# Expert layers: weights stationary in the first layer of two-tile units, plain transposes and a VectorE sum for half tiles

## The chip, the cores and the metric

The kernel runs on one core of one Trainium2 chip. The metric is the device time of one execution in microseconds (us), as the median of several runs. The engines are TensorE (PE, with its weight loads shown as PEld), VectorE (DVE), ScalarE (ACT), GpSimd (POOL) and SyncE (SP, which here only issues DMAs).

## The reference, cut to what matters

Three stages run one after another: clustered attention, a dense layer with a PReLU, and a mixture of eight experts. Only the last is touched:

```python
def _moe2_ref(x, w_skip, w_gate, w1, w2):
    do_compute = x @ w_skip > 0
    xc = x[do_compute]
    e_idx = np.argmax(xc @ w_gate, axis=1)          # one expert per token
    ...
    for e in range(E):                              # E = 8, w1[e]: 512x1024, w2[e]: 1024x512
        mask = e_idx == e
        h = np.maximum(xc[mask] @ w1[e], 0.0)
        y[mask] = gate_w[mask, None] * (h @ w2[e])
    out[do_compute] = xc + y                        # the other tokens keep x
```

## The kernel before

**Precision.** Every fp32 operand of a large matmul is split into a high part and a low part (tiles that end in `h` and `l`), and a product is three matmuls: high by high, high by low, low by high. The split of a weight chunk is a ScalarE copy (`Weights.hi`, L1453) and then a VectorE subtraction (`Weights.lo`, L1457), each over 128x2048 elements. The low part of an activation is made in the same way: ScalarE writes the high part, VectorE subtracts.

**Units and tiles.** Tokens are sorted by expert and cut into units. A unit shares the four weight chunks of one expert: c = 0 and 1 are the two 512-column halves of the first layer, chunks 2 and 3 those of the second layer. In the order of work there are ten units, 0 to 9, with 16 tiles: a full tile has 128 tokens, a half tile 64. Units 2, 4 and 6 hold two full tiles (tiles 3 and 4, 6 and 7, 9 and 10). Units 1, 3 and 5 hold one half tile (tiles 2, 5, 8), units 0, 7 and 9 a full and a half one (the half ones are tiles 1, 12, 15), unit 8 one full one. A further block of nine units follows under a condition that these inputs do not meet.

**One tile.** Written as function calls, with t the tile and c the half:

- `transx(t)`: four TensorE transposes of the gathered rows `xg` into a PSUM bank `pt` (L1152, L1159 for half tiles), a ScalarE copy to the high part, a VectorE subtraction to the low part. In a half tile, high and low stand side by side in one 128-column operand, so that two groups of matmuls do instead of three, and the two halves of the result have to be added.
- `first(t, c)`: `group` (L1197) issues 12 matmuls (8 for a half tile). The token tile is the stationary operand and the weights move, 512 columns each; the result `h` has tokens on its partitions. ScalarE then writes `hb` (L1226).
- `transh(t, c)`: `hb` is transposed for the second layer. A full tile takes four transposes (L1242), a ScalarE copy `hTh` (L1243) and a VectorE subtraction `hTl` (L1250). A half tile takes four fp32 matmuls with the constant `two`, which transpose and add the two halves at once (L1238; the profile shows each as two instructions), a ScalarE relu (L1239) and a VectorE step (L1247).
- `second(t, c)`: 12 matmuls (8) with `hT` stationary into `yo`; after c = 1 the output is scaled and scattered.

**What sets the order.** Nothing reorders the instructions: each engine has its own queue and works through it in the order in which the code is written. `begin` writes out units 0 to 2 by hand, interleaved with the last part of the routing; `run` writes the rest by a rule. A turn is one `first` or `second`. At the start of a turn `ahead` converts one more weight chunk if one of the five slots is free (a `hi` on ACT, a `lo` on DVE) and has POOL issue the load of that chunk for the unit after the next. Then come the matmuls, then `transh` of the turn before, then the `transx` of the next unit. For a unit of one tile the turns are first(0), first(1), the first turn of the next unit, second(0), second(1):

```python
            if use and wsp.slots and n > 1:
                ahead()
            if c < 2:
                first(t, c)
            else:
                second(t, c - 2)
            while wait:
                transh(*wait.pop(0))
            if c < 2:
                wait.append((t, c))
```

**PSUM.** The pool `t` has three banks in rotation (transposes use it), `h` two, `y` two. A write into a bank waits until the last reader of its former contents is through.

Of the kernel before, what the change touches and what calls it, by code (L numbers as in the profile page):

```python
# [8 lines left out]
F32 = mybir.dt.float32  # L9
F32R = mybir.dt.float32r  # L10
# [16 lines left out]
DM = H * D  # L27
# [16 lines left out]
HALF = P // 2  # L44
# [25 lines left out]
TILES, UNIT, COLS = _plan()  # L70
# [15 lines left out]
HT = 4  # L86
# [1081 lines left out]
def moe2(ctx, tc, A, cst, R, y1d, wsp, wk, op, ps, x0, route, room):  # L1168
    nc = tc.nc
    ident = cst["ident"]  # L1170
    KD = DM // P
    xg, xT, hb, hT, yo, hp, more = {}, {}, {}, {}, {}, {}, []
    for t in range(2):
        xg[t], xT[t] = x0[0][t], (x0[1][0], x0[1][1:])[t]

    def gather(t):

# [29 lines left out]
    def is_half(t):  # L1207
        return TILES[t][2] < P

    def transx(t):  # L1210
        pt = ps["t"].tile([P, 4, P], F32, tag="t", name="pt")
        xT[t] = [wk.tile([P, 4, P], F32R, tag=f"xT{y}", name=f"xT{y}") for y in "hl"]
        if not is_half(t):
            transpose_x(nc, ident, xg[t], pt, *xT[t])
            return
        transpose_half(nc, ident, xg[t], pt, xT[t][0], TILES[t][1])

    def first(t, c, ks=range(4)):
        n = TILES[t][0]
        if ks[0] == 0:  # L1220
            hp[t, c] = ps["h"].tile([P, DM], F32, tag="h", name="h")
        group(hp[t, c], xT[t], wsp.w[n, c], is_half(t), True, True, ks)
        if ks[-1] == KD - 1:
            done(n, c)
            r = wk.tile([P, DM], F32, tag="hb", name="hb")
            nc.scalar.activation(r, hp.pop((t, c)), AF.Copy if is_half(t) else AF.Relu)  # L1226
            hb[t, c] = r

    def transh(t, c, late=None):
        pt = ps["t"].tile([P, 4, P], F32, tag="t", name="pt")  # L1230
        r = hb.pop((t, c))
        a = wk.tile([P, 4, P], F32R, tag="hTh", name="hTh", bufs=HT)
        b = wk.tile([P, 4, P], F32R, tag="hTl", name="hTl", bufs=HT)
        hT[t, c] = (a, b)
        if is_half(t):

            for k in range(4):
                nc.tensor.matmul(pt[:, k, :HALF], lhsT=r[:, k * P:(k + 1) * P], rhs=R["two"], start=True, stop=True)  # L1238
            nc.scalar.activation(a[:, :, :HALF], pt[:, :, :HALF], AF.Relu)  # L1239
        else:  # L1240
            for k in range(4):
                nc.tensor.transpose(pt[:, k], r[:, k * P:(k + 1) * P], ident)  # L1242
# [114 lines left out]
    def run(n0, n1, fresh=False):  # L1357


        tiles = {n: list(UNIT[n]) for n in range(n0, n1)}  # L1360
        F = {n: [(t, c) for c in range(2) for t in tiles[n]] for n in tiles}
        turns = []
        for n in range(n0, n1):
            if fresh or n > n0:
                turns += F[n]
            if len(tiles[n]) == 1 and 1 < n < n1 - 1:
                turns.append(F[n + 1].pop(0))
            if n + 1 < n1:
                turns += [(t, 2 + c) for c in range(2) for t in tiles[n]]
            else:  # L1370

                turns += [(t, 2 + c) for t in reversed(tiles[n]) for c in range(2)]
        use = []
        for t, c in turns:
            if (TILES[t][0], c) not in use and (TILES[t][0], c) not in wsp.w:
                use.append((TILES[t][0], c))

        def ahead():
            n, c = use.pop(0)
            wsp.take(n, c)  # L1380
            wsp.hi(n, c)
            wsp.lo(n, c, nc.vector)
            if n + 2 < n1:
                loadw(n + 2, c)

        last = UNIT[n1 - 1][-1] + 1
        if fresh:
            for t in range(UNIT[n0][0], UNIT[n0][0] + sum(XG)):
                gather(t)
            for n in (n0, n0 + 1):  # L1390
                for c in range(NPC):
                    loadw(n, c)
            for t in tiles[n0]:
                transx(t)
        wait = []
        for t, c in turns:
            n = TILES[t][0]
# [10 lines that stand above are left out]
            if c < 2 and n + 1 < n1:  # L1408

                if len(tiles[n]) == 1:  # L1410
                    rows = tiles[n + 1][c:c + 1]
                else:
                    rows = tiles[n + 1] if (t, c) == (tiles[n][-1], 1) else ()
                for t2 in rows:
                    transx(t2)
            if use and wsp.slots and n == 1:
                ahead()
            if c == 3:
                finish(t)
                if t + sum(XG) < last:  # L1420
                    gather(t + sum(XG))
# [39 lines left out]
def kernel(ctx, tc, A):  # L1461
    nc = tc.nc
# [4 lines left out]
    ident = cp.tile([P, P], F32, name="ident")  # L1467
# [20 lines left out]
    R = {}  # L1488
# [5 lines left out]
    def setup(sp):  # L1494
# [116 lines left out]
    wsp = Weights(nc, A, slots, raw)  # L1611
# [19 lines left out]
    def more():  # L1631
        rp2 = ctx.enter_context(tc.tile_pool(name="rawp2", bufs=1, reuse_waits="tile"))
        raw.extend(rp2.tile([P, 2048], F32, name=f"raw{c}") for c in (2, 3))
        R["pool"] = rp2

        pre = [rp2.tile([P, 2048], F32, tag=f"pre{c}", name=f"pre{c}") for c in range(NW)]
        for f in range(3, DFF // P):
            w32[f] = pre[(f - 2) // 2][:, (f % 2) * 2 * DM:(f % 2 + 1) * 2 * DM]
        xg = [rp2.tile([P, DM + 1], F32, name=f"xg{t}") for t in range(2)]
        place = iter(range(NW // 2))  # L1640

        def last():
# [17 lines left out]
        return fwk, fck, ps_y, wsp, slot, last, even, xg, setup  # L1660
# [16 lines left out]
    ps = {}  # L1677
# [60 lines left out]
```

## Time and profile before

| what | value |
|---|---|
| runs | 735.36 us median of 3 (734.87 to 736.76) |
| profiled execution, its own time | 735.44 us |
| its span (first to last instruction) | 733.5 us |
| PE busy | 707.3 us (96%) |
| DVE busy | 566.0 us (77%) |
| ACT busy | 477.9 us (65%) |
| expert stage | from about 532 us to the end of the span |

The span is what the profile shows; the 1.9 us between it and the execution's own time lie outside. Busy shares are averages over stages with different limits, so the expert stage has to be read by itself. In a timeline each row is one instruction or several equal ones that follow each other: start, length, engine, line, operation, tile written and tiles read, shapes, count, and in brackets how long the engine stood idle before it and what ended that.

### The profile page before, as it was taken

The page shows a single profiled execution, that of the slowest core. Times are in us where ns is not written, and L with a number is a line of the kernel's source. Part 1 is how long each engine was busy: PE and PEld are TensorE (multiplying, and loading weights), DVE is VectorE, ACT ScalarE, POOL GpSimd, SP SyncE. Part 2 cuts the span into 40 slices and gives each one's busy share as a digit, 9 for nine tenths or more (in the row PEclk, how much of TensorE's full clock was granted, in tenths as well). Part 3 has the DMA queues.
Part 4 walks back from the last instruction along what each step waited for, and adds up shares of the span by engine and source line. Part 5 has one row for each costly group of instructions (what it writes and reads, how often), then busy time and mean ns, then how long its engine had stood idle before and what let it go on. Part 6 is the DMA issues. An engine that isn't in the chain of part 4 may idle for free. (4 is left out here: it accounts for less than half of the span.)

```text
span 733.5 us, 11633 instructions
## 1 busy us (share of the span) xinstructions
PE 707.3 (96%) x4022; PEld 623.9 (85%) x4022; DVE 566.0 (77%) x1110; ACT 477.9 (65%) x916; POOL 375.0 (51%) x340
## 2 busy tenths in 40 slices
PE   9999999999999999999999999999999999999993
PEld 6988999889999899888889999998888778888872
DVE  5989888798989877888875989875478887775731
ACT  5878898788899955554446555656446676665620
POOL 4649778797796386666660000001127776583101
PEclk9999999999999999999999999999999999999997
DMA  7876668576656133333306200142618896867000
GB/s 210 226 170 170 125 134 198 146 176 128 172 144 155 52 110 126 116 115 115 115 0 210 93 2 0 58 109 111 241 44 314 313 404 247 321 226 304 18 10 25
DMA packets 46162, 109.22 MB, mean 149 GB/s; under 512 B 10779, under 2 KB 26587, under 8 KB 40721
## 3 DMA queue, kind: packets, MB, share of 16 engines
q1 hardware_dynamic: 39024, 67.81, 34.2%
q0 software_dynamic: 7072, 40.60, 14.7%
q8 instruction: 34, 0.56, 0.3%
q14 instruction: 32, 0.25, 0.1%
HBM read 74.78 MB, written 10.10 MB: 116 GB/s over the span
## 5 line engine op out<-in xcount | busy, mean ns | idle before, releaser
L341 DVE TENSOR_TENSOR etl<-pt,eth 128x384 fp32r<-128x384 f32 x192 | 102.2, 550 | 21.8 <-ACT eth L340 20.3
L340 ACT CAST eth<-pt 128x384 fp32r<-128x384 f32 x192 | 91.1, 486 | 20.4 <-PE pt L338 20.4
L338 PE MATMUL pt<-ident,e 128*128 128x128 f32 x576 | 93.7, 272 | 0.3 <-ACT e L327 0.3
L320 DVE TENSOR_REDUCE nm<-s 128x1 f32<-128x768 f32 x96 | 90.5, 943 | 3.2 <-PE s L307 2.9
L1165 POOL DMA_INDIRECT xg<-y1d,gi x16 | 26.3, 1646 | 130.1 <-DVE gi L1014 113.8
L327 ACT ACTIVATE e<-s,nm 128x768 f32<-128x768 f32 x96 | 87.5, 911 | 4.4 <-DVE nm L320 3.7
L695 ACT CAST gh<-gm 128x384 fp32r<-128x384 f32 x60 | 30.8, 514 | 82.0 <-DVE gm L693 58.5
L338 PEld LDWEIGHTS pt<-ident,e 128*128 128x128 f32 x576 | 73.6, 140 | 7.0 <-ACT e L327 0.5
L697 DVE TENSOR_TENSOR gl<-gm,gh 128x384 fp32r<-128x384 f32 x60 | 49.4, 823 | 25.7 <-ACT gh L695 25.1
L356 PE MATMUL px<-etl,vh 128*64 128x384 f32 (+1 forms) x192 | 65.7, 369 | 1.1 <-DVE etl L341 0.9
L304 PE MATMUL s<-AB 128*128 128x384 f32 x192 | 57.5, 380 | 2.3 <-ACT e L327 2.0
L667 PE MATMUL h<-xh,wh 128*128 128x384 f32 x256 | 55.8, 339 | 0.6 <-DVE gm L690 0.4
L667 PE MATMUL h<-xh,wl 128*128 128x384 f32 x256 | 56.0, 339 | 0.0
L567 POOL TENSOR_TENSOR pre<-ct,pre 128x512 int32<-128x512 int32 x26 | 37.2, 1453 | 35.9 <-DVE ct L565 35.9
L1285 POOL DMA_INDIRECT out_dram<-o,si x16 | 20.5, 1280 | 68.4 <-DVE o L1280 40.4
L667 PE MATMUL h<-xl,wh 128*128 128x384 f32 x256 | 55.0, 336 | 0.0
L358 PE MATMUL px<-eth,vh 128*128 128x384 f32 x160 | 53.9, 337 | 0.0
L1457 DVE TENSOR_TENSOR wl<-raw,wh 128x2048 fp32r<-128x2048 f32 (+2 forms) x26 | 44.3, 1712 | 11.6 <-ACT wh L1453 11.3
L307 PE MATMUL s<-CD 128*128 128x384 f32 x192 | 49.4, 338 | 1.0 <-DMA CD<-st 1.0
L667 PEld LDWEIGHTS h<-xh,wh 128*128 128x128 f32 x256 | 45.6, 188 | 3.3 <-DVE gm L690 0.5
L667 PEld LDWEIGHTS h<-xh,wl 128*128 128x128 f32 x256 | 44.6, 188 | 2.6 <-POOL wl L639 2.5
L667 PEld LDWEIGHTS h<-xl,wh 128*128 128x128 f32 x256 | 45.8, 188 | 0.0
(344 smaller groups left out, 1836.7 us busy)
## 6 DMA issues: line engine op xcount, KB each, us to landing
AB<-RL SPq DMA_DIRECT2D x32, 384.0 KB, 5.2
raw<-in_w_in_dram SPq DMA_DIRECT2D x16, 512.0 KB, 4.0
raw<-in_w_out_dram SPq DMA_DIRECT2D x16, 512.0 KB, 4.8
raw<-in_wall_dram SPq DMA_DIRECT2D x8, 1024.0 KB, 8.1
Tp<-in_qkT_dram SPq DMA_DIRECT2D x16, 384.0 KB, 3.7
CD<-RL SPq DMA_DIRECT2D x16, 384.0 KB, 6.5
raw<-in_wall_dram POOLq DMA_DIRECT2D x4, 1024.0 KB
vt<-in_v_dram SPq DMA_DIRECT2D x8, 384.0 KB, 6.1
```

The lines of the kernel that those rows point to most:

```text
L304: nc.tensor.matmul(s[:, u, :384], lhsT=AB[:, 0, t * P:(t + 1) * P], rhs=AB[:, 1, ks], start=True, stop=False)
L307: nc.tensor.matmul(s[:, u, :384], lhsT=CD[:, 0, t * P:(t + 1) * P], rhs=CD[:, 1, ks], start=False, stop=True)
L320: nc.vector.tensor_reduce(out=nm, in_=s[:, :, :384], axis=AX.XY, op=ALU.max, negate=True)
L327: nc.scalar.activation(e.rearrange("p (u c) -> p u c", u=2), s[:, :, :384], AF.Exp, bias=nm, accum_out=den[:, i % 3:i % 3 + 1])
L338: nc.tensor.transpose(pt[:, i2], e[:, kt * P:(kt + 1) * P], ident)
L340: nc.scalar.copy(eh, pt)
L341: lows[u] = lambda: nc.vector.tensor_tensor(out=etl[:, 3 * u:3 * u + 3, q * P:(q + 1) * P], in0=pt, in1=eh.bitcast(F32), op=ALU.subtract)
L356: nc.tensor.matmul(px[:m], lhsT=vh[:, kt, :m], rhs=etl[:, kt], start=False, stop=False)
L358: nc.tensor.matmul(px, lhsT=vh[:, kt, :], rhs=eth[:, kt], start=False, stop=(kt == NT - 1))
L667: nc.tensor.matmul(hs[c], lhsT=a[:, k * P:(k + 1) * P], rhs=x[:, k, c * HC:(c + 1) * HC], start=(k == 0 and i == 0), stop=(k == KD - 1 and ...
L697: eng.tensor_tensor(out=gl[:, o], in0=m, in1=gh[:, o].bitcast(F32), op=ALU.subtract)
L1457: eng.tensor_tensor(out=lo[:, a:b], in0=self.src(t, c)[:, a:b], in1=hi[:, a:b].bitcast(F32), op=ALU.subtract)
```

## The change

Three edits, all in the expert stage.

1. In units of two full tiles (2, 4, 6) the first layer is turned round. `wide` makes the weights the stationary operand and moves both token tiles together, 256 columns. One turn makes two of the four 128-row blocks of the transposed hidden layer for both tiles: 24 matmuls of 256 columns in place of 12 of 512. The result already stands transposed, so that `transh` has no transposes for these units: ScalarE writes the relu straight to the high part, and `transh` only issues the VectorE step for the low part. The result bank comes from the pool `t`, no longer from `h`. Both `transx` of such a unit now come right after the first turn of the unit before it.
2. In half tiles `transh` uses four plain transposes, a VectorE reduction that adds the two halves (written over `hb`), the relu on ScalarE from there, and the low part on VectorE.
3. Buffers follow: the high and low parts stand in tiles of 256 columns, the half tiles' `xT` in one fixed place, and the constant `two` goes.

```diff
+    def wide(t, c):
+        n = TILES[t][0]
+        (xh, xl), (wh, wl) = xT[n, "wide"], wsp.w[n, c]
+        if t == UNIT[n][0]:
+            hT[n, c] = [both("hT", HT) for _ in "hl"]
...
+        d0 = 2 * UNIT[n].index(t)
+        h = ps["t"].tile([P, 2, 2 * P], F32, tag="t", name="hw")
+        for d in range(2):
+            for i, (w, x) in enumerate(((wh, xh), (wh, xl), (wl, xh))):
+                for k in range(4):
+                    o = k * DM + (d0 + d) * P
+                    nc.tensor.matmul(h[:, d], lhsT=w[:, o:o + P], rhs=x[:, k], start=(i + k == 0), stop=(i == 2 and k == 3))
+        done(n, c)
+        a, b = (y[:, d0:d0 + 2] for y in hT[n, c])
+        nc.scalar.activation(a, h, AF.Relu)
+        hb[t, c] = lambda: nc.vector.scalar_tensor_tensor(out=b, in0=h, scalar=0.0, in1=a.bitcast(F32), op0=ALU.max, op1=ALU.subtract)

     def first(t, c, ks=range(4)):
         n = TILES[t][0]
+        if is_wide(n):
+            return wide(t, c)
...
     def transh(t, c, late=None):
+        r = hb.pop((t, c))
+        if is_wide(TILES[t][0]):
+            return r()
         pt = ps["t"].tile([P, 4, P], F32, tag="t", name="pt")
...
+        for k in range(4):
+            nc.tensor.transpose(pt[:, k], r[:, k * P:(k + 1) * P], ident)
         if is_half(t):
-
-            for k in range(4):
-                nc.tensor.matmul(pt[:, k, :HALF], lhsT=r[:, k * P:(k + 1) * P], rhs=R["two"], start=True, stop=True)
-            nc.scalar.activation(a[:, :, :HALF], pt[:, :, :HALF], AF.Relu)
+            g = r[:, :4 * HALF].rearrange("p (k m) -> p k m", k=4)
+            nc.vector.tensor_reduce(out=g, in_=pt.rearrange("p k (s m) -> p k m s", s=2), axis=AX.X, op=ALU.add)
+            nc.scalar.activation(a[:, :, :HALF], g, AF.Relu)
         else:
-            for k in range(4):
-                nc.tensor.transpose(pt[:, k], r[:, k * P:(k + 1) * P], ident)
             nc.scalar.copy(a, pt)
...
-                    rows = tiles[n + 1][c:c + 1]
+                    rows = tiles[n + 1] if is_wide(n + 1) and c == 0 else () if is_wide(n + 1) else tiles[n + 1][c:c + 1]
```

How the queues change is shown at unit 5 (tile 8, a half tile, before unit 6 with tiles 9 and 10); unit 3 before unit 4 has the same pattern. First VectorE, from the low part of unit 5's last chunk on. Before:

```order
L1457 TENSOR_TENSOR lastl<-raw_3823,lasth 128x2048
L1154 TENSOR_TENSOR xTl<-pt,xTh 128x512
L1457 TENSOR_TENSOR wl_5969<-even_6291,wh_5968 128x2048
L1247 SCALAR_TENSOR_TENSOR hTh<-pt,hTh 128x4x64
L1154 TENSOR_TENSOR xTl<-pt,xTh 128x512
L1457 TENSOR_TENSOR wl_5614<-even_6542,wh_5613 128x2048
L1247 SCALAR_TENSOR_TENSOR hTh<-pt,hTh 128x4x64
L1250 TENSOR_TENSOR hTl<-pt,hTh 128x512
L1457 TENSOR_TENSOR wl_6541<-even_6543,wh_6540 128x2048
```

After the change, the same stretch (`hw` is the result of the turned first layer; L1502 is the `lo` of a weight chunk, L1285 the new reduction, L1292 the low part of a half tile):

```order
L1502 TENSOR_TENSOR lastl<-raw_3823,lasth 128x2048
L1154 TENSOR_TENSOR xT<-pt,xT 128x4x128 x2
L1502 TENSOR_TENSOR wl_5967<-even_6289,wh_5966 128x2048
L1285 TENSOR_REDUCE hb<-pt 128x256
L1292 SCALAR_TENSOR_TENSOR hT<-hb,hT 128x4x64
L1502 TENSOR_TENSOR wl_5615<-even_6540,wh_5614 128x2048
L1285 TENSOR_REDUCE hb<-pt 128x256
L1292 SCALAR_TENSOR_TENSOR hT<-hb,hT 128x4x64
L1255 SCALAR_TENSOR_TENSOR hT<-hw,hT 128x512
L1502 TENSOR_TENSOR wl_6539<-even_6541,wh_6538 128x2048
```

The two subtractions of `xT` now stand together ahead of the second chunk, and each low part of the half tile has a reduction ahead of it.

ScalarE in the same stretch, from the `hb` of the half tile's first turn to the fourth chunk. Before:

```order
L1226 ACTIVATE hb<-h 128x512
L1153 CAST xTh<-pt 128x512
L1453 CAST wh_5968<-even_6291 128x2048
L1226 ACTIVATE hb<-h 128x512
L1239 ACTIVATE hTh<-pt 128x4x64
L1153 CAST xTh<-pt 128x512
L1453 CAST wh_5613<-even_6542 128x2048
L1226 ACTIVATE hb<-h 128x512
L1239 ACTIVATE hTh<-pt 128x4x64
L1243 CAST hTh<-pt 128x512
L1453 CAST wh_6540<-even_6543 128x2048
```

After the change (L1498 is the `hi` of a weight chunk, L1286 the relu of the half tile, which now reads `hb`, where the reduction wrote; L1254 the relu of the turned layer):

```order
L1267 ACTIVATE hb<-h 128x512
L1153 CAST xT<-pt 128x4x128 x2
L1498 CAST wh_5966<-even_6289 128x2048
L1267 ACTIVATE hb<-h 128x512
L1286 ACTIVATE hT<-hb 128x4x64
L1498 CAST wh_5614<-even_6540 128x2048
L1254 ACTIVATE hT<-hw 128x512
L1286 ACTIVATE hT<-hb 128x4x64
L1498 CAST wh_6538<-even_6541 128x2048
```

The relu of the half tile stands in the same place between two chunks as before; it now reads VectorE's result instead of PSUM. The copy `hTh` of the next unit's first turn (L1243) is gone.

TensorE at the same place, from the half tile's first turn to the second layer of its first half. Before:

```order
L1197 MATMUL h<-wh_5968,xTh 128x512 x4
L1197 MATMUL h<-wl_5969,xTh 128x512 x4
L1152 MATMUL pt<-ident,xg 128x128 x4
L1197 MATMUL h<-wh_5613,xTh 128x512 x4
L1197 MATMUL h<-wl_5614,xTh 128x512 x4
L1238 MATMUL pt<-two,hb 128x64 x4
L1152 MATMUL pt<-ident,xg 128x128 x4
L1197 MATMUL h<-wh_6289,xTh 128x512 x4
L1197 MATMUL h<-wl_6290,xTh 128x512 x4
L1197 MATMUL h<-wh_6289,xTl 128x512 x4
L1238 MATMUL pt<-two,hb 128x64 x4
L1197 MATMUL yo<-wh_6540,hTh 128x512 x4
```

After:

```order
L1198 MATMUL h<-wh_5966,lastl 128x512 x4
L1198 MATMUL h<-wl_5967,lastl 128x512 x4
L1152 MATMUL pt<-ident,xg 128x128 x8
L1198 MATMUL h<-wh_5614,lastl 128x512 x4
L1198 MATMUL h<-wl_5615,lastl 128x512 x4
L1282 MATMUL pt<-ident,hb 128x128 x4
L1251 MATMUL hw<-xT,wh_6287 128x256 x8
L1251 MATMUL hw<-xT,wl_6288 128x256 x4
L1251 MATMUL hw<-xT,wh_6287 128x256 x8
L1251 MATMUL hw<-xT,wl_6288 128x256 x4
L1282 MATMUL pt<-ident,hb 128x128 x4
L1198 MATMUL yo<-wh_6538,hT 128x512 x4
```

The eight transposes of the next unit's two tiles stand together, and the 12 matmuls of 512 columns between the two transposes of the half tile are 24 of 256.

## Rows read from the trace of the kernel before

**Rows 1.** Busy time by stretch: us and instructions of each engine, granted clock, DMA.

```profile
590.00:605.00 15.00, 13.95 (x73) 11.25 (x72) 14.52 (x12) 11.55 (x13) 11.22 (x6) 1.00 1.01 421
...
605.00:640.00 35.00, 35.00 (x175) 28.91 (x174) 25.97 (x23) 23.20 (x25) 21.84 (x14) 1.00 0.79 299
```

**Rows 2.** Timeline of weight loads (PEld): start us, us, tile, idle before. Unit 5, others.

```profile
628.78 0.89 PEld L1197 LDWEIGHTS h<-wh,xTh 128*128 128x128 f32 x4
...
637.03 1.09 PEld L1238 LDWEIGHTS pt<-two,hb 128*128 128x128 f32 x8
...
638.04 0.77 PEld L1197 LDWEIGHTS yo<-wh,hTh 128*128 128x128 f32 x4
...
642.09 0.89 PEld L1197 LDWEIGHTS h<-wh,xTh 128*128 128x128 f32 x4
...
644.89 0.89 PEld L1197 LDWEIGHTS h<-wh,xTh 128*128 128x128 f32 x4
...
651.47 0.47 PEld L1152 LDWEIGHTS pt<-ident,xg 128*128 128x128 f32 x4
...
651.91 0.47 PEld L1159 LDWEIGHTS pt<-ident,xg 128*128 128x128 f32 x4
```

**Rows 3.** Timeline of weight loads, 384-column matmuls of the stage before.

```profile
420.35 0.71 PEld L667 LDWEIGHTS h<-xh,wh 128*128 128x128 f32 x4
...
422.43 1.28 PEld L716 LDWEIGHTS y<-wh,gh 128*128 128x128 f32 x6
```

**Rows 4.** Timeline of ScalarE in unit 5.

```profile
629.21 1.90 ACT L1453 CAST lasth<-raw 128x2048 fp32r<-128x2048 f32 x1 [3.71 <-PE yo L1197]
...
632.10 1.92 ACT L1453 CAST wh<-even 128x2048 fp32r<-128x2048 f32 x1
...
634.39 0.40 ACT L1239 ACTIVATE hTh<-pt 128x256 fp32r<-128x256 f32 x1
...
635.15 1.93 ACT L1453 CAST wh<-even 128x2048 fp32r<-128x2048 f32 x1
...
638.30 0.39 ACT L1239 ACTIVATE hTh<-pt 128x256 fp32r<-128x256 f32 x1 [0.18 <-PE pt L1238]
```

**Rows 5.** Timeline of VectorE in unit 5.

```profile
634.06 2.29 DVE L1457 TENSOR_TENSOR wl<-even,wh 128x2048 fp32r<-128x2048 f32 x1
...
637.20 2.28 DVE L1457 TENSOR_TENSOR wl<-even,wh 128x2048 fp32r<-128x2048 f32 x1
...
639.40 0.42 DVE L1247 SCALAR_TENSOR_TENSOR hTh<-pt,hTh 128x256 fp32r<-128x256 f32 x1
```

**Rows 6.** VectorE reductions, by line and shape: count, busy, mean ns of one.

```profile
L320 DVE TENSOR_REDUCE nm<-s 128x1 f32<-128x768 f32 x96 | 90.5, 943 | 3.2 <-PE s L307 2.9
...
L1098 DVE TENSOR_REDUCE rs<-yts 128x48 f32<-128x384 f32 x1 | 0.6, 553 | 0.0
```

**Rows 7.** Timeline: unit 2 and the load for unit 4.

```profile
565.13 2.29 DVE L1457 TENSOR_TENSOR wl<-even,wh 128x2048 fp32r<-128x2048 f32 x1 [1.37 <-ACT wh L1453]
...
578.92 0.68 DVE L1250 TENSOR_TENSOR hTl<-pt,hTh 128x512 fp32r<-128x512 f32 x1
...
588.54 1.90 ACT L1453 CAST wh<-even 128x2048 fp32r<-128x2048 f32 x1 [6.56 <-DMA even<-in_wall_dram,wi]
...
590.35 0.58 ACT L1243 CAST hTh<-pt 128x512 fp32r<-128x512 f32 x1
...
593.42 0.76 PEld L1197 LDWEIGHTS yo<-wh,hTl 128*128 128x128 f32 x4 [0.75 <-DVE hTl L1250]
```

**Rows 8.** The end: timeline of weight loads and matmuls, then clock by stretch.

```profile
713.40 0.76 PEld L1197 LDWEIGHTS yo<-wh,hTh 128*128 128x128 f32 x4 [1.07 <-DVE hTh L1247]
...
720.05 1.10 PE L1197 MATMUL yo<-wh,hTl 128*128 128x512 f32 x4
...
724.00:726.00 2.00, 0.00 (x0) 0.00 (x0) 0.00 (x0) 0.00 (x0) 0.00 (x0) 0.99 0.24 88
...
726.00:728.00 2.00, 0.00 (x0) 0.00 (x0) 0.00 (x0) 0.00 (x0) 0.00 (x0) 0.50 0.02 4
```

More of the change, by code (lines that the diff above doesn't have):

```diff
@@ L1173, in moe2 @@
     for t in range(2):
-        xg[t], xT[t] = x0[0][t], (x0[1][0], x0[1][1:])[t]
+        xg[t], xT[t] = x0[0][t], (x0[1][0], x0[1][1:2])[t]
+    xs = x0[1][2]
     def gather(t):
@@ L1208, in is_half, with is_wide, side, both @@
         return TILES[t][2] < P
+    def is_wide(n):
+        return sum(TILES[t][2] for t in UNIT[n]) == 2 * P
+    def side(t):
+        return slice(UNIT[TILES[t][0]].index(t) * P, (UNIT[TILES[t][0]].index(t) + 1) * P)
+    def both(tag, bufs):
+        return wk.tile([P, 4, 2 * P], F32R, tag=tag, name=tag, bufs=bufs)
     def transx(t):
+        n = TILES[t][0]
         pt = ps["t"].tile([P, 4, P], F32, tag="t", name="pt")
-        xT[t] = [wk.tile([P, 4, P], F32R, tag=f"xT{y}", name=f"xT{y}") for y in "hl"]
-        if not is_half(t):
-            transpose_x(nc, ident, xg[t], pt, *xT[t])
+        if is_half(t):
+            xT[t] = [xs]
+            transpose_half(nc, ident, xg[t], pt, xs, TILES[t][1])
             return
-        transpose_half(nc, ident, xg[t], pt, xT[t][0], TILES[t][1])
+        if is_wide(n):
+            if t == UNIT[n][0]:
+                xT[n, "wide"] = [both("xT", 2) for _ in "hl"]
+            xT[t] = [x[:, :, side(t)] for x in xT[n, "wide"]]
+        else:
+            x = both("xT", 2)
+            xT[t] = x[:, :, :P], x[:, :, P:]
+        transpose_x(nc, ident, xg[t], pt, *xT[t])
+    def wide(t, c):
+        n = TILES[t][0]
+        (xh, xl), (wh, wl) = xT[n, "wide"], wsp.w[n, c]
+        if t == UNIT[n][0]:
+            hT[n, c] = [both("hT", HT) for _ in "hl"]
+            for t2 in UNIT[n]:
+                hT[t2, c] = [h[:, :, side(t2)] for h in hT[n, c]]
+        d0 = 2 * UNIT[n].index(t)
[9 more added lines that the diff above has]
+        hb[t, c] = lambda: nc.vector.scalar_tensor_tensor(out=b, in0=h, scalar=0.0, in1=a.bitcast(F32), op0=ALU.max, op1=ALU.subtract)
     def first(t, c, ks=range(4)):
         n = TILES[t][0]
+        if is_wide(n):
+            return wide(t, c)
         if ks[0] == 0:
@@ L1229, in transh @@
     def transh(t, c, late=None):
+        r = hb.pop((t, c))
+        if is_wide(TILES[t][0]):
+            return r()
         pt = ps["t"].tile([P, 4, P], F32, tag="t", name="pt")
-        r = hb.pop((t, c))
-        a = wk.tile([P, 4, P], F32R, tag="hTh", name="hTh", bufs=HT)
-        b = wk.tile([P, 4, P], F32R, tag="hTl", name="hTl", bufs=HT)
+        if c == 0 or not is_half(t):
+            hT[t] = both("hT", HT)
+        a, b = hT[t][:, :, :P], hT[t][:, :, P:]
+        if is_half(t):
+            a = (a, b)[c]
         hT[t, c] = (a, b)
+        for k in range(4):
+            nc.tensor.transpose(pt[:, k], r[:, k * P:(k + 1) * P], ident)
         if is_half(t):
-            for k in range(4):
-                nc.tensor.matmul(pt[:, k, :HALF], lhsT=r[:, k * P:(k + 1) * P], rhs=R["two"], start=True, stop=True)
-            nc.scalar.activation(a[:, :, :HALF], pt[:, :, :HALF], AF.Relu)
-        else:
-            for k in range(4):
-                nc.tensor.transpose(pt[:, k], r[:, k * P:(k + 1) * P], ident)
+            g = r[:, :4 * HALF].rearrange("p (k m) -> p k m", k=4)
+            nc.vector.tensor_reduce(out=g, in_=pt.rearrange("p k (s m) -> p k m s", s=2), axis=AX.X, op=ALU.add)
+            nc.scalar.activation(a[:, :, :HALF], g, AF.Relu)
+        else:
             nc.scalar.copy(a, pt)
@@ L1246, in low @@
             if is_half(t):
-                nc.vector.scalar_tensor_tensor(out=a[:, :, HALF:], in0=pt[:, :, :HALF], scalar=0.0, in1=a[:, :, :HALF].bitcast(F32),
+                nc.vector.scalar_tensor_tensor(out=a[:, :, HALF:], in0=g, scalar=0.0, in1=a[:, :, :HALF].bitcast(F32),
                                                op0=ALU.max, op1=ALU.subtract)
@@ L1558, in setup @@
         yield
-        two = R["two"] = R["pool"].tile([P, HALF], F32, name="two")
-        nc.vector.tensor_tensor(out=two, in0=ident[:, :HALF], in1=ident[:, HALF:], op=ALU.add)
-        yield
         R["p0"] = R["pool"].tile([P, 1], F32, name="p0")
@@ L1646, in last @@
             xT = x[0][:, 2048:].rearrange("p (i k m) -> p i k m", i=2, k=DM // P)
-            return (xT[:, 0], xT[:, 1]), x[1][:, 2048:2048 + 4 * P].rearrange("p (k m) -> p k m", k=DM // P)
+            return (xT[:, 0], xT[:, 1]), *(x[1][:, o:o + 4 * P].rearrange("p (k m) -> p k m", k=DM // P) for o in (2048, 2048 + 4 * P))
         def even(c):
```

## The prediction

> **What bounds the kernel now.** I read busy time by stretch first, then the timelines of the weight loads, ScalarE and VectorE in the expert stage. TensorE is busy in all 35.00 us from 605 to 640 at full clock, while VectorE is busy in 25.97; just before, from 590 to 605, VectorE is busy in 14.52 of 15.00 and TensorE in 13.95 [rows 1]. So most of the stage runs at TensorE's pace, and the stretches around the half units are nearly VectorE's. Both facts matter, because the change takes work from TensorE and gives some to VectorE, in the half units above all.
>
> The waits in unit 2 are of another kind. ScalarE stood idle 6.56 us until 588.54 for the load of unit 4's first chunk; the copy queued behind that conversion ran only at 590.35, and TensorE waited for the low part of tile 4 until 593.42 [rows 7]. Work saved before that point comes to nothing unless the load comes earlier.
>
> **TensorE's terms.** Twelve matmuls of 512 columns take 644.89 - 642.09 = 2.80 us, 0.233 each [rows 2]. Twelve of 384 columns take 422.43 - 420.35 = 2.08 us, 0.173 each [rows 3]. No row has 256 columns in this precision. Upper bound: the 0.173 of 384 columns with the same weight load. Lower bound: four transposes issued behind four others took 651.91 - 651.47 = 0.44 us [rows 2], 0.11 each, which is the closest that fp32 weight loads stand here. The line through 512 and 384 gives 0.233 - 2 x 0.060 = 0.113; the share by which both exceed columns/2.4 GHz (9% and 8%) gives 0.116. I take 0.118, near the lower bound, since two fits of the same instruction point there. A wide turn is then 24 x 0.118 = 2.83 us, 0.03 more than now, and it saves four transposes, 0.44. Net -0.4 for each of 12 turns.
>
> A half tile's transposition takes 638.04 - 637.03 = 1.01 us, of which 0.12 comes back, since the four loads behind it take 0.77 and not 0.89 [rows 2]: 0.89 against 0.44 for four plain transposes. Net -0.45 for each of 12. If nothing waited, the sum would be 12 x 0.4 + 12 x 0.45 = 10.2 us less.
>
> **ScalarE and VectorE.** ScalarE loses a copy per wide turn, which costs or gives nothing by itself. VectorE's low part of a wide turn takes the place of `hTl`, 0.68 us [rows 7], at about the same cost. New are 12 reductions of 512 elements from PSUM. Between 0.553 us for 384 elements and 0.943 for 768 [rows 6], which are also the bounds, the line gives 0.68.
>
> The size of the reduction is the smaller part. It is the place. Before, a half tile's relu on ScalarE needed only TensorE, so ScalarE ran ahead of VectorE by a chunk. Now the relu needs the reduction, which stands on VectorE behind a `lo` of 2.29 us; the next `hi` stands behind the relu on ScalarE; the next `lo` needs that `hi`; and the second reduction stands behind that `lo`. The two engines take turns.
>
> **Unit 5 step by step**, with T = 628.78, the start of tile 8's first matmul [rows 2]. The first `hi` waits for TensorE and starts at T + 0.43 either way [rows 4].
>
> - The second `hi` started at T + 3.32 [rows 4]; one copy of `xT` more (about 0.5) stands ahead of it now: T + 3.8 to T + 5.7.
> - Its `lo`: T + 5.8 to T + 8.1 (before T + 5.28, 2.29 long) [rows 5].
> - First reduction to T + 8.7; relu, 0.40 [rows 4], to T + 9.15; low part, 0.42 [rows 5], to T + 9.6.
> - The third `hi` can start only behind that relu: T + 9.1 to T + 11.0. Before it started at T + 6.37 [rows 4].
> - Its `lo`: T + 11.0 to T + 13.3 (before T + 8.42) [rows 5]. Second reduction to T + 13.9, relu to T + 14.4, low part to T + 14.85. Before, this low part ended at T + 11.04 [rows 5].
>
> TensorE alone would need 2 x 1.87 for `first` (8 x 0.233), 0.88 for the eight transposes, 2 x 0.44, 2.83, and 1.87 for `second(8,0)`, so that `second(8,1)` could start at T + 10.2. It has to wait until T + 14.9 and ends at T + 16.75. Before it ended at 642.09 = T + 13.31 [rows 2]. So the half unit and the first wide turn that lies in it cost 3.45 us more, in spite of the 1.3 us that were saved in it. About 0.8 us of the idle time comes ahead of `second(8,0)` and 3.4 ahead of `second(8,1)`. Behind them queue tile 9's second turn and all of unit 6. Unit 3, ahead of unit 4, has the same order on all three engines: 3.45 once more. The low part on VectorE, not the weights, is what is late.
>
> **Unit 2 and the routing.** Two reductions with their relus (tile 2) come ahead of the `lo` that started at 565.13 [rows 7]; one of them lies under other work, the other delays it by 0.68 and a hop, about 0.9. Everything behind it on VectorE moves along, and with it the output of tile 1, after whose scatter POOL issues the load on which ScalarE waited until 588.54: +0.9 at the end of unit 2, with a lower bound of 0 (the earlier TensorE could pull the chain) and an upper of 2 (both reductions). The fourth wide turn also needs the bank of the first, which comes free only after the low part of 578.92 to 579.60 [rows 7], moved by 0.9: TensorE stands about 4.7 us there, under the cover of the load. The reductions of tile 1 lie in the routing, where one stands ahead of the gather's indices; TensorE has work there, and I cost it at 0 (0.7 if that cover is gone).
>
> **The rest.** Units 4 and 6 have three wide turns each outside the half units: 2 x 3 x -0.4 = -2.4. Unit 7's half tile has `hTl` and slack around it: 2 x -0.45 = -0.9. Unit 9's is the same, but `second(15,1)` follows its transposition directly and already waited 1.07 us [rows 8]; reduction and hop add 0.8: -0.1.
>
> Sum: 0.9 + 3.45 + 3.45 - 2.4 - 0.9 - 0.1 = +4.4. On the profiled execution's 735.44 us (0.08 above the median of the runs shown): **739.8 us**.
>
> **What holds the ring together.** The forecast needs VectorE and ScalarE to keep strictly to their order. The copy at 590.35, ready long before but run behind the conversion that waited for a load [rows 7], shows that for ScalarE. The Trainium skill says it as well (TensorE: Matmul & The Clock Gate, Architectural detail): only TensorE reorders, and there only weight loads; ScalarE and VectorE take their queues strictly in turn. If they did not, the relu's wait would not hold the `hi` back and the sum would be that of the first rival.
>
> **Rivals.**
>
> - *Faster: the ring does not close.* If the conversions ran about 4.6 us earlier against TensorE (T + 14.85 against T + 10.2; two of them are 4.4), `second(8,1)` would not wait, and units 3 and 5 would give 1.2 us each instead of costing 3.45. Sum 0.9 - 2.4 - 2.4 - 1.0 = -4.9: 730.5, and down to 725.2 if nothing waits in unit 2 either. For it: from 605 on VectorE has a quarter of its time free [rows 1]. Against: the first `hi` waits for TensorE, so it cannot start sooner [rows 4]. It decides at one chunk: with half of the lead the result is about 735.
> - *About the same: half of the ring.* One of the two conversions is out of the way, 2.2 us per half unit: 4.4 - 4.4 = 0, 735.4.
> - *Slower still: the clock falls.* After the last matmul (720.05 to 721.15) the granted clock was 0.99 in 724 to 726 and 0.50 (1.2 GHz) from 726 [rows 8], so after some 4.8 us without work. The stall of 4.7 us in unit 2 is near that. At half the clock the wide turn behind it takes 2.8 us more; with the two stalls of 3.4 us the same could come three times: 742.6 to 748. The Trainium skill (same page, HAM oscillation) warns that a TensorE left idle falls back to its lower clock; that it does so at the end agrees, whether these shorter stalls suffice no row shows.
> - *Slower still: 256 columns cost as much as 384.* Six wide turns lie in the open: 6 x 24 x 0.055 = 7.9, giving 747.7. For it: the recorded loads last 0.19 us, longer than 0.118. Against: the records overlap, as the transposes show.
>
> **How the numbers follow.** A measurement of this kernel can tell about 0.3% (2.2 us) from no change. Chances: the forecast 50% (737.6 to 742), faster 19%, half of the ring 14%, clock 10%, slow matmuls 7%. Slower by more than that: 67%; faster 20%; within 13%. The range of 731 to 746 leaves out the lower part of the fast rival (12%) and the slow matmuls with the far end of the clock (8%).
>
> **What would show it.** The 256-column matmuls start 0.11 to 0.13 us apart. In unit 5 the third `hi` starts right behind the half tile's relu, and TensorE waits some 3 us for L1292 ahead of `second(8,1)`; the same in unit 3. In unit 2 TensorE waits for a bank ahead of the fourth wide turn. Units 4, 6 and 7 are shorter. I am wrong if TensorE does not wait ahead of the half tiles' second layer, or if the 256-column matmuls stand further apart.

## The result: slower by 10.4 us, and the profile after

| what | before | after |
|---|---|---|
| runs | 735.12 us median of 4 (734.7 to 736.76) | 745.57 us median of 4 (744.94 to 746.33) |
| ratio of times | | 1.0139, 95% from 1.0115 to 1.0163 |
| profiled execution, its span, mean granted clock | 735.44, 733.5 us, 0.993 | 745.83, 743.9 us, 0.982 |

The forecast was 739.8 us: the direction was right, the loss was more than twice the +4.4 us that the sum gave. First the busy time by stretch after the change, with the columns of [rows 1]:

```profile
565.00:590.00 25.00, 20.12 (x129) 18.49 (x128) 18.23 (x14) 15.43 (x16) 16.67 (x13) 0.93 0.84 312
590.00:605.00 15.00, 14.35 (x77) 11.75 (x76) 11.99 (x9) 8.66 (x8) 10.93 (x6) 1.00 1.01 418
605.00:620.00 15.00, 11.21 (x65) 9.54 (x65) 10.22 (x11) 9.22 (x10) 9.47 (x7) 0.89 0.58 215
620.00:640.00 20.00, 20.00 (x111) 17.13 (x110) 13.70 (x12) 10.47 (x11) 9.93 (x8) 1.00 0.94 346
640.00:660.00 20.00, 16.11 (x93) 14.13 (x92) 14.50 (x14) 10.84 (x11) 11.05 (x8) 0.83 0.70 257
```

In [rows 1] TensorE had no gap between 605 and 640. Now 3.8 of the 15 us from 605 are idle, and 3.9 of the 20 us from 640; between them, in the body of unit 4, there is still no gap. The clock, which was 1.00 in all of these stretches, is below 1 in three of them. Next the timeline of weight loads after the change, with the stalls in units 2, 3 and 5 (the turned turns are L1251, the other layers L1198):

```profile
580.35 1.20 PEld L1251 LDWEIGHTS hw<-xT,wh 128*128 128x128 f32 x8 [4.51 <-DVE hT L1255]
...
592.51 0.42 PEld L1198 LDWEIGHTS yo<-wh,hT 128*128 128x128 f32 x2
594.01 1.23 PEld L1198 LDWEIGHTS yo<-wh,hT 128*128 128x128 f32 x6 [1.08 <-DVE hT L1255]
...
597.15 0.89 PEld L1198 LDWEIGHTS h<-wh,lastl 128*128 128x128 f32 x4
...
612.06 1.35 PEld L1198 LDWEIGHTS yo<-wh,hT 128*128 128x128 f32 x4 [3.53 <-DVE hT L1292]
...
615.22 1.15 PEld L1251 LDWEIGHTS hw<-xT,wh 128*128 128x128 f32 x8
...
616.76 1.02 PEld L1251 LDWEIGHTS hw<-xT,wh 128*128 128x128 f32 x8
...
618.19 1.01 PEld L1251 LDWEIGHTS hw<-xT,wh 128*128 128x128 f32 x8
...
635.42 0.88 PEld L1198 LDWEIGHTS h<-wh,lastl 128*128 128x128 f32 x4
...
645.09 0.76 PEld L1198 LDWEIGHTS yo<-wh,hT 128*128 128x128 f32 x4 [0.93 <-DVE hT L1292]
...
650.39 1.36 PEld L1198 LDWEIGHTS yo<-lasth,hT 128*128 128x128 f32 x4 [3.62 <-DVE hT L1292]
...
653.55 1.61 PEld L1251 LDWEIGHTS hw<-xT,wh 128*128 128x128 f32 x6
...
656.28 0.90 PEld L1251 LDWEIGHTS hw<-xT,wh 128*128 128x128 f32 x7
...
675.31 0.65 PEld L1198 LDWEIGHTS h<-lasth,xT 128*128 128x128 f32 x3
...
724.06 0.76 PEld L1198 LDWEIGHTS yo<-wh,hT 128*128 128x128 f32 x4 [1.99 <-DVE hT L1292]
```

The reader is to see four things. First, twelve matmuls of 256 columns take 618.19 - 616.76 = 1.43 us, 0.119 each, as forecast. Second, TensorE waits 3.53 and 3.62 us for L1292 ahead of the half tiles' second half, as forecast. Third, what comes behind these waits is slow: `second(8,1)` takes 653.55 - 650.39 = 3.16 us, and the next twelve matmuls of 256 columns 656.28 - 653.55 = 2.73. The same two pieces take 1.75 and 1.53 us in e4 below, where the clock stays at 1.00. Fourth, in unit 2 the wait at 594.01 stands in the middle of a `second`, with 14 matmuls (3.14 us) behind it.

To compare piece by piece, three boundaries of the timeline before are needed beside those of [rows 2, 7] and the last four matmuls of [rows 8]: the first matmul of the expert stage, the end of unit 3's half tile and the end of unit 6.

```profile
532.48 0.19 PEld L1197 LDWEIGHTS h<-wh,lasth 128*128 128x128 f32 x1
...
607.53 0.66 PEld L1197 LDWEIGHTS h<-wh,xTh 128*128 128x128 f32 x3
...
663.70 0.41 PEld L1197 LDWEIGHTS h<-lasth,xTh 128*128 128x128 f32 x2
```

After the change the first of these starts at 531.94, and the last four matmuls, in the timeline of TensorE after it, at 730.71:

```profile
730.71 1.09 PE L1198 MATMUL yo<-wh,hT 128*128 128x512 f32 x4
```

| piece | before | after | difference | forecast |
|---|---|---|---|---|
| up to the first matmul | 532.48 | 531.94 | -0.54 | 0 |
| to tile 5's first matmul (end of unit 2) | 61.75 | 65.21 | +3.46 | +0.9 |
| unit 3's half tile | 13.30 | 18.07 | +4.77 | +3.45 |
| rest of unit 4 | 21.25 | 20.20 | -1.05 | -1.2 |
| unit 5's half tile | 13.31 | 18.13 | +4.82 | +3.45 |
| rest of unit 6 | 21.61 | 21.76 | +0.15 | -1.2 |
| units 7 to 9 | 56.35 | 55.40 | -0.95 | -1.0 |
| sum | | | +10.66 | +4.4 |

The -0.54 lies in stages that the change does not touch; the same boundary stands at 534.52 in the profiled execution of e5 below, so it says nothing.

**The ring.** The timeline of ScalarE after the change, the late load of unit 2 and unit 5:

```profile
589.13 1.91 ACT L1498 CAST wh<-even 128x2048 fp32r<-128x2048 f32 x1 [3.25 <-DMA even<-in_wall_dram,wi]
...
639.14 1.93 ACT L1498 CAST wh<-even 128x2048 fp32r<-128x2048 f32 x1
...
644.17 0.42 ACT L1286 ACTIVATE hT<-hb 128x256 fp32r<-128x256 f32 x1 [2.60 <-DVE hb L1285]
644.49 1.89 ACT L1498 CAST wh<-even 128x2048 fp32r<-128x2048 f32 x1
...
649.40 0.42 ACT L1286 ACTIVATE hT<-hb 128x256 fp32r<-128x256 f32 x1 [2.52 <-DVE hb L1285]
```

And that of VectorE, the same places:

```profile
591.06 2.29 DVE L1502 TENSOR_TENSOR wl<-even,wh 128x2048 fp32r<-128x2048 f32 x1 [4.73 <-ACT wh L1498]
593.27 0.68 DVE L1255 SCALAR_TENSOR_TENSOR hT<-hw,hT 128x512 fp32r<-128x512 f32 x1
...
641.19 2.28 DVE L1502 TENSOR_TENSOR wl<-even,wh 128x2048 fp32r<-128x2048 f32 x1
643.39 0.68 DVE L1285 TENSOR_REDUCE hb<-pt 128x256 f32<-128x512 f32 x1
...
646.41 2.29 DVE L1502 TENSOR_TENSOR wl<-even,wh 128x2048 fp32r<-128x2048 f32 x1 [1.37 <-ACT wh L1498]
648.62 0.68 DVE L1285 TENSOR_REDUCE hb<-pt 128x256 f32<-128x512 f32 x1
649.84 0.50 DVE L1292 SCALAR_TENSOR_TENSOR hT<-hb,hT 128x256 fp32r<-128x256 f32 x1 [0.54 <-ACT hT L1286]
```

Read the two side by side from 641.19: `lo`, reduction, relu (after 2.60 us idle on ScalarE), `hi` (right behind it, 644.49), `lo` (after 1.37 us idle on VectorE), reduction, relu (2.52 idle), low part. In [rows 4, 5] neither engine waited for the other here, and the low part ended at T + 11.04. With T = 635.42 now, the third `hi` starts at T + 9.07 (forecast T + 9.1), its `lo` at T + 10.99 (T + 11.0), and the low part ends at T + 14.92 (T + 14.85).

**The clock.** Windows of the execution after the change, around the stall in unit 5:

```profile
646.00:648.00 2.00, 1.21 (x6) 0.65 (x4) 1.59 (x1) 0.87 (x2) 1.50 (x2) 1.00 0.52 140
648.00:650.00 2.00, 0.00 (x0) 0.00 (x0) 1.46 (x3) 0.60 (x2) 1.70 (x2) 0.84 0.88 274
650.00:651.00 1.00, 0.60 (x2) 0.51 (x3) 0.94 (x2) 1.00 (x1) 0.88 (x1) 0.50 0.99 393
...
655.00:656.00 1.00, 1.00 (x7) 1.00 (x6) 0.96 (x2) 1.00 (x1) 0.18 (x1) 0.50 0.96 401
656.00:657.00 1.00, 1.00 (x10) 1.00 (x10) 0.66 (x2) 0.60 (x1) 0.43 (x1) 0.91 1.03 393
```

TensorE ran out of work at about 647.2 (1.21 us busy from 646). The granted clock fell to 0.50, 1.2 GHz, within 648 to 650, and stayed there until shortly after 656, over `second(8,1)` and the first twelve matmuls of tile 10's turn, the second of unit 6.

### The profile page after: what moved, and what is told of

Same layout as the page of the kernel before. It is cut to its first block, busy times and chain, and to the rows that moved or that the text cites. A ratio compares the mean times of both kernels' runs of the same rounds, so it can differ in the third digit from the quotient of the medians.

```text
span 743.9 us, 11696 instructions
## 1 busy us (share of the span) xinstructions
PE 705.1 (95%) x4070; PEld 625.4 (84%) x4070; DVE 574.8 (77%) x1121; ACT 471.2 (63%) x904; POOL 364.3 (49%) x340
## 5 line engine op out<-in xcount | busy, mean ns | idle before, releaser
L1165 POOL DMA_INDIRECT xg<-y1d,gi x16 | 24.0, 1501 | 130.3 <-DVE gi L1014 113.8
L1502 DVE TENSOR_TENSOR wl<-raw,wh 128x2048 fp32r<-128x2048 f32 (+2 forms) x26 | 44.4, 1714 | 13.8 <-ACT wh L1498 13.3
L1198 PE MATMUL yo<-wh,hT 128*128 128x512 f32 x144 | 40.5, 409 | 7.6 <-DVE hT L1292 7.0
## 6 DMA issues: line engine op xcount, KB each, us to landing
raw<-in_wall_dram POOLq DMA_DIRECT2D x4, 1024.0 KB, 10.4
```

The lines of the kernel that those rows point to most:

```text
L1502: eng.tensor_tensor(out=lo[:, a:b], in0=self.src(t, c)[:, a:b], in1=hi[:, a:b].bitcast(F32), op=ALU.subtract)
```

## The experiments

Every experiment starts from the changed kernel unless it says otherwise, and is compared with the kernel before on the same chip: e1 to e4 beside a median of 735.33 us (19 runs), e5 to e7 beside 735.32 (29), e8 and e9 beside 736.88 (23).

**e1, the turned layer alone.** Half tiles go back to the matmuls with `two`, a constant that is made again; no reduction.

```diff
         if is_half(t):
-            g = r[:, :4 * HALF].rearrange("p (k m) -> p k m", k=4)
-            nc.vector.tensor_reduce(out=g, in_=pt.rearrange("p k (s m) -> p k m s", s=2), axis=AX.X, op=ALU.add)
+            for k in range(4):
+                nc.tensor.matmul(pt[:, k, :HALF], lhsT=r[:, k * P:(k + 1) * P], rhs=R["two"], start=True, stop=True)
+            g = pt[:, :, :HALF]
             nc.scalar.activation(a[:, :, :HALF], g, AF.Relu)
```

> The first layer of the two-tile units is turned as in the change; the half tiles keep the matmuls with the constant that adds the halves (no VectorE reduction). Theory (ring: reduction behind a weight chunk on VectorE, next chunk's copy behind the relu on ScalarE): units 3 and 5 fall back to about 13 us each, no low clock before the end, units 4 and 6 keep their gain of about 1.1 us each; unit 2 still ends about 2.3 us later, since the second layer of tile 3 needs the blocks of both turns and so the low part behind the late load. Sum about -0.6: 734 to 736. Rival (the turned layer itself is what costs, by its bank and by the blocks that both tiles share): stays near the changed kernel, 742 to 746.

Measured 735.49 us (734.38 to 736.69, 10 runs), ratio 1.0006 (0.9992 to 1.0021). The stalls in units 3 and 5 are gone; what stays is the wait for a bank in unit 2, in its timeline of weight loads:

```profile
580.45 1.78 PEld L1251 LDWEIGHTS hw<-xT,wh 128*128 128x128 f32 x8 [4.69 <-DVE hT L1255]
```

The granted clock is 0.86 over 565 to 590. From the end of unit 2 to tile 8's first matmul it takes 630.65 - 597.49 = 33.16 us; before, 628.78 - 594.23 = 34.55 [rows 2]. So the turned layer gains there 1.39 us in four turns, where -0.4 for each was costed, and gives it back in unit 2, which ends 2.64 us later, counted from the first matmul of the stage.

**e2, the half tiles alone.**

```diff
     def is_wide(n):
-        return sum(TILES[t][2] for t in UNIT[n]) == 2 * P
+        return False
```

> Only the half tiles are changed (plain transposes, VectorE reduction); the two-tile units keep the layer of before. Theory (ring): units 3 and 5 take about 18 us each as in the changed kernel, with TensorE waiting over 3 us for the half tile's low part and half the clock behind it: 743 to 747. Rival (the turned layer costs): the half tiles' saved TensorE time comes through, 730 to 735.

Measured 745.35 us (743.64 to 746.73, 4 runs), ratio 1.0153 (1.0128 to 1.0178): the half tiles alone lose all of it. In its timeline of weight loads the two stalls stand without any turned layer:

```profile
610.11 1.02 PEld L1198 LDWEIGHTS yo<-wh,hT 128*128 128x128 f32 x4 [2.92 <-DVE hT L1292]
...
649.48 0.76 PEld L1198 LDWEIGHTS yo<-lasth,hT 128*128 128x128 f32 x4 [2.92 <-DVE hT L1292]
```

**e3, the ring opened.** Everything of the change, but VectorE's `lo` of the next chunk, and the load behind it, are issued after `transh` of the turn before. For this `ahead` hands them back as the function `low`; that part of the edit is left out here.

```diff
-            if use and wsp.slots and n > 1:
-                ahead()
+            low = ahead() if use and wsp.slots and n > 1 else None
...
             while wait:
                 transh(*wait.pop(0))
+            if low:
+                low()
```

> The changed kernel with one thing moved: in each turn the VectorE part of the next weight chunk (and the load behind it) is issued after the hidden layer's transposition of the turn before, no longer ahead of the matmuls. The reduction then stands ahead of the chunk. Theory (ring): the half tile's second low part is ready about 10.9 us after the unit's start and not 14.9, units 3 and 5 take some 13 us, the clock stays high, the wait for the bank in unit 2 shrinks: 731 to 735. Rival (the reduction and the turned layer cost by their length, not their place): 743 to 746.

Measured 735.09 us (733.61 to 737.94, 10 runs), ratio 1.0004 (0.9986 to 1.0022): 10.5 us less than the change, from the place of VectorE's `lo` and of the load behind it alone, though just outside the range expected. Unit 2 now ends 1.18 us earlier than before, counted as above. The clock is 1.00 in every stretch from 565 to 660. In its timeline of weight loads the half units still wait a little:

```profile
600.77 1.07 PEld L1251 LDWEIGHTS hw<-xT,wh 128*128 128x128 f32 x8 [1.51 <-ACT hb L1267]
...
606.64 0.77 PEld L1198 LDWEIGHTS yo<-wh,hT 128*128 128x128 f32 x4 [0.83 <-DVE hT L1292]
```

1.51 + 0.83 us in unit 3, and nearly the same in unit 5, is more than the 0.9 that the plain transposes save in a half tile. The pieces of the table above now take 608.39 - 594.06 = 14.33 us in unit 3 and 642.79 - 628.44 = 14.35 in unit 5, still 1.03 and 1.04 more than before, where the change had 4.77 and 4.82.

**e4, the clock held up.** The change, with extra matmuls that nobody reads in the three stalls: 30 ahead of `wide(4,1)`, 22 each ahead of `second(5,1)` and `second(8,1)`.

```diff
+            keep({(4, 1): 30, (5, 3): 22, (8, 3): 22}.get((t, c), 0))
             if c < 2:
                 first(t, c)
...
+    def keep(count):
+        if count:
+            x = ps["r"].tile([P, 288], F32, tag="r", name="keep")
+        for _ in range(count):
+            nc.tensor.matmul(x, lhsT=cst["identb"], rhs=R["low"].rearrange("p a b c -> p (a b c)"), start=True, stop=True)
```

> The changed kernel with extra matmuls into an unused bank in the three long stalls of TensorE (30 ahead of the fourth turned matmul group of unit 2, 22 ahead of the second layer of the half tiles' second half in units 3 and 5); their results are read by nobody. Theory (the clock fell in the stalls, at about 1.3 us for each stall of units 3 and 5 and 1.3 more at the start of unit 6): the granted clock stays at 1.0 up to the end and 3 to 4 us come back, 741 to 743. Rival (the stalls alone are the loss): no change against the changed kernel, 745 to 746.

Measured 741.62 us (740.73 to 742.32, 4 runs), ratio 1.0094 (1.007 to 1.0118): 3.95 us less than the change, with more work on TensorE. The clock is 1.00 from 565 to 660. This is the price of the slow clock; the 6.3 us that are left over the kernel before are those of the waits, less what the change saves. Its timeline of weight loads gives unit 3's slow pieces at full clock, and shows that unit 2 has another cause:

```profile
594.05 1.22 PEld L1198 LDWEIGHTS yo<-wh,hT 128*128 128x128 f32 x6 [1.52 <-DVE hT L1255]
...
612.09 0.77 PEld L1198 LDWEIGHTS yo<-wh,hT 128*128 128x128 f32 x4 [0.70 <-DVE hT L1292]
...
613.84 1.13 PEld L1251 LDWEIGHTS hw<-xT,wh 128*128 128x128 f32 x8
...
615.37 1.02 PEld L1251 LDWEIGHTS hw<-xT,wh 128*128 128x128 f32 x8
```

`second(5,1)` takes 613.84 - 612.09 = 1.75 us and the twelve matmuls behind it 1.53; in unit 5 the same two take 650.74 - 648.99 = 1.75 and 652.27 - 650.74 = 1.53.

With the clock up, the wait inside `second(3,1)` only grows, from 1.08 to 1.52 us, and tile 5's first matmul starts at 597.18 where it started at 597.15: the whole 3.9 us between the two spans (743.9 and 740.0) lie behind unit 2. One reservation: counted from the first matmul of the stage (533.04 here) unit 2 ends 1.07 us earlier than in the change, since the load that it waits for was under way 1.1 us less; that differs between executions.

**e5 and e6, unit 2's bank, then also the low part later.** e5 is e1 with the first turn of each pair put into the pool `h`, so that no turn waits for a bank; e6 is e5 with `lo` moved as in e3.

```diff
-        h = ps["t"].tile([P, 2, 2 * P], F32, tag="t", name="hw")
+        p = "th"[d0 == 0]
+        h = ps[p].tile([P, 2, 2 * P], F32, tag=p, name="hw")
```

> As the run with the turned layer alone, and the result of the first tile's turn takes its bank from the pool of two that the turned units no longer use, so that the fourth turn waits for no bank. Theory (in unit 2 the second layer of tile 3 already waits for the low part of the fourth turn, which stands behind the chunk that waits for the late load): the stall of 4.7 us ahead of the fourth turn and the low clock behind it are gone, and unit 2 still ends near 596.5, 2.3 us later than before; 734 to 735.5. Rival (the bank and the clock are all that unit 2 loses): unit 2 ends at 594.2 or earlier, 731.5 to 733.

> As the run before, and the VectorE part of the next chunk is issued after the hidden layer's transposition of the turn before. Theory: the low part of the fourth turn now stands ahead of the chunk that waits for the load, so that unit 2 ends near 593.7; units 3 and 5 gain 0.4 us each and units 4 and 6 1.1 each: 731 to 733, faster than both kernels. Rival (unit 2 is held by the load itself): unit 2 ends near 596.5, as in the run before.

e5 measured 734.35 us (731.58 to 736.75, 12 runs), ratio 0.9985 (0.9963 to 1.0007). The bank wait is gone, and its 4.7 us are not gained. The timeline of weight loads of e5:

```profile
584.47 1.24 PEld L1198 LDWEIGHTS yo<-lasth,hT 128*128 128x128 f32 x6 [1.90 <-DVE hT L1256]
...
594.28 1.23 PEld L1198 LDWEIGHTS yo<-wh,hT 128*128 128x128 f32 x6 [4.36 <-DVE hT L1256]
```

The low part of the fourth turn stands on VectorE at 593.55, behind the `lo` of the late chunk (591.34), and unit 2 ends 2.70 us later than before counted from the first matmul, as it did with the bank wait. Part of this is the clock: it is 0.89 over 590 to 605, and the 14 matmuls behind the 4.36 us take 598.97 - 594.28 = 4.69 us where they took 3.14 in the change. e6 measured 733.94 us (731.8 to 735.15, 12 runs), ratio 0.9974 (0.9954 to 0.9994), somewhat above what was expected. With the low part ahead of that `lo`, unit 2 ends 4.77 us earlier than before by the same count. The time comes back at the next thing that stands behind the late load; the timeline of e6:

```profile
600.51 0.91 PEld L1252 LDWEIGHTS hw<-xT,wh 128*128 128x128 f32 x4 [3.58 <-DVE xT L1154]
```

Here the low part of `xT` waits in VectorE's queue behind three `lo`s, the first of them again that of the late chunk, whose `hi` started at 589.31 after 8.91 us of waiting for the load. The clock is 0.89 in that stretch.

**e7, the low part later, banks as in the change** (e1 with the edit of e3).

> The turned layer alone, with the VectorE part of the next chunk moved as in the run before, and the banks as in the change. Theory: the wait for the bank is shorter than 4.7 us, since the first turn's low part no longer stands behind two chunks (2.3 us in the run that moved the chunk in the changed kernel), the clock holds, and the wait is covered: 731 to 733.5. Rival (the bank costs in full): 734 to 736.

Measured 733.7 us (732.85 to 736.16, 12 runs), ratio 0.9979 (0.996 to 0.9999), slightly slower than expected. Between e3 and e7 only the half tiles differ: e7, without plain transposes, is not slower, 733.7 against 735.09.

**e8 and e9, the load earlier.** e8 is e6 with unit 4's first load issued ahead of POOL's scatter and gathers; e9 is the kernel before with that edit alone.

```diff
+        loadw(4, 0)
         scatter(1, output(1))
         for t in range(6, sum(XG) + 2):
             gather(t)
-        loadw(4, 0)
```

> The turned layer with the other bank and the later VectorE part, and the load of unit 4's first chunk issued ahead of the scatter of tile 1 and the three gathers behind it, some 6 us earlier. Theory (what is left of the gain in unit 2 is lost to that late load, on which the next conversions and, behind them, the low parts of unit 4's tokens wait, 3.6 us of TensorE in the run before): that wait goes, 730 to 732. Rival (the load arrives no sooner, since the DMA engines are full there): no change, 733 to 735.

> The kernel before with only that load issued earlier. Theory: its own wait of 1.9 us at the end of unit 2 goes: 733 to 734. Rival (DMA engines full): no change, 735 to 736.

e8 measured 733.9 us (730.65 to 735.98, 12 runs), ratio 0.9968 (0.9949 to 0.9988). The load came sooner: its `hi` starts 582.50 - 532.91 = 49.59 us after the first matmul of the stage, against 589.31 - 533.79 = 55.52 in e6. The wait in unit 3 is gone, but one of 2.70 us for `xT` (L1154) stands in unit 5 at 631.75 with a clock of 0.83 from 620 to 640, so the 730 to 732 expected were not reached. e9 measured 735.39 us (median of 12, one of which, at 998.33 us, stands far apart and is not in the ratio), ratio 0.9994 (0.9971 to 1.0016): the waits at the end of unit 2 are gone from its timeline, and no gain could be measured. In the profiled execution the gain is there: from the first matmul of the stage to the last four weight loads it takes 719.01 - 533.61 = 185.40 us, against 719.82 - 532.48 = 187.34 before. The other runs, 733.9 to 739.0 us, spread over more than these 1.9 us, so whether a gain of that size is in them stays open. e6, e7 and e8 are 0.2 to 0.3% faster than the kernel before; the upper ends of their intervals (0.9988 to 0.9999) are close to no change, and the intervals do not tell the three apart.

## Why the forecast had the sign and not the size

**Right: the prices.** 256-column matmuls 0.119 us (forecast 0.118); the reduction 0.685 us, mean of twelve (0.68); the wait for a bank in unit 2 4.51 us (4.7), that in unit 9 1.99 us where 1.07 [rows 8] and 0.8 were expected. The group in the change:

```profile
L1285 DVE TENSOR_REDUCE hb<-pt 128x256 f32<-128x512 f32 x12 | 8.2, 685 | 3.7 <-PE pt L1282 3.7
```

**Right: the ring, place and size.** Without the slow `second` (3.16 - 1.75 = 1.41, with the 1.75 of e4), units 3 and 5 cost 3.36 and 3.41 us more; the forecast was 3.45 for each. One step of it does not add up: `second(8,0)` could start at T + 8.33 by the prediction's own terms and had to wait until T + 9.6, which is 1.3 us and not 0.8; the profile shows 0.93 there, and the sum does not use the figure. And what it calls tile 9's second turn is tile 10's turn, by the order of `run`. That the ring is the cause, and not the turned layer or its buffers, is shown three ways: the turned layer alone has no stall (e1), the half tiles alone have it (e2), and moving VectorE's `lo` behind the low part leaves 1.0 us of it in each half unit (e3). This also refutes the two rivals in which the ring closes not at all or by half.

**Right: the rest.** Units 4 and 7 to 9 came within 0.15 us of their terms, and so does unit 6 once its 2.73 - 1.53 = 1.20 us at the slow clock are taken off.

**Wrong: the clock, left out of the sum as a rival at 10%.** The stalls were forecast at 3.4 us, and 3.53 and 3.62 us were enough for the clock to fall. It cost 1.41 us behind unit 3's stall (the half layer; the twelve matmuls behind it, 616.76 - 615.22 = 1.54, are at the 1.53 of e4), and 1.41 and 1.20 behind unit 5's: 4.0 us, which e4 confirms with 3.95 less. The third fall, in unit 2, shows in no piece, since TensorE waited behind it anyway. The 2.8 us a fall of that rival were right for unit 5 (2.6) and twice too much for unit 3 (1.4). The step that failed is that the sum put this term at nothing, and a tenth of the chances on it, with the 4.8 us at the end of the program [rows 8] as its only row; here 3.5 us of waiting were enough. The Trainium skill (TensorE: Matmul & The Clock Gate, HAM oscillation) describes a kernel in which TensorE waits between bursts and each next burst starts at the lower clock; the rows of units 3 and 5 above agree with it, while in e2's unit 5 a wait of 2.92 us left the clock at 1.00.

**Wrong: unit 2, mis-sized at +0.9, measured +3.46.** The step was "two reductions with their relus (tile 2) come ahead of the `lo`", with the bank wait under the cover of the load. That part has about its size: counted from the first matmul, POOL issues the late load 580.82 - 531.94 = 48.88 us on and not 580.13 - 532.48 = 47.65, 1.23 later, and the `hi` of the late chunk starts at 57.19 us (589.13 - 531.94) and not at 56.06 (588.54 - 532.48), 1.13 later. It is not the same in every execution: in e4 the load is issued 1.26 us later than before, and its `hi` starts only 0.06 later (589.16 - 533.04 = 56.12). What was missed is that a turned turn makes blocks for both tiles, and tile 3's `second(3,1)` reads blocks of tile 4's turn. Before, only tile 4's own second layer waited for the low part behind the late load, and four matmuls were left behind that wait at 593.42 [rows 7]. Now 14 are, and ten matmuls at 0.233 us are the other 2.33 of the 3.46. e4 (no slow clock) and e5 (no bank wait) both keep the wait, e6 (low part ahead of the `lo`) loses it. In e1 a like 2.6 us come from the bank wait and the slow turn behind it, so two causes of like size lie side by side there, and taking away one of them (e5, where the wait for the low part and the slow clock behind it take its place) gains nothing in unit 2.

Of the 6.26 us that the forecast fell short (10.66 - 4.4), the clock is 4.02, unit 2 is 2.56, the other terms together 0.22, less the 0.54 ahead of the stage.

## What to carry to other kernels

When a step moves onto one of two engines that already pass work to each other, write out both queues in order, with the waits between them: the reduction's 0.68 us cost 3.4 us a time through the order of the queues, and moving the next chunk's low part behind it left 1.0 us of that. When an operand is made for two consumers at once, look at the earlier consumer, which now waits for the later one's inputs. And here a stall of some 3 us on TensorE had to be priced with the slow work behind it, not by its length alone.

## What was unexpected of the hardware

The clock did not fall after a fixed idle time. In the change it fell some 2.2 us after the last matmul's end in unit 5 (647.2; 0.84 over 648 to 650 puts the fall at 649.4), against 4.8 us at the end of the kernel before [rows 8]. In e2 the same stall of 2.92 us was followed by a granted clock below 1 in unit 3 and by 1.00 in unit 5, as its windows show:

```profile
605.00:620.00 15.00, 12.12 (x49) 9.29 (x48) 11.07 (x10) 10.33 (x12) 8.08 (x4) 0.89 0.51 178
...
640.00:660.00 20.00, 16.60 (x76) 12.88 (x75) 16.56 (x14) 12.12 (x14) 12.87 (x7) 1.00 0.70 266
```

By the idle time of the weight loads in the expert stage, which in unit 5 of the change begins at 646.77, 0.4 us before the last matmul ends, stalls up to 2.33 us (e3, e7) left it at 1.00, and those of 3.5 us or more were all followed by a clock below 1. Between them the runs show both.
